# A shared pool of eight PSUM banks, one-instruction Q evacuation and ordered loads in a fused attention and token-MLP kernel

## The chip, the cores and the metric

The kernel runs on one core of a Trainium2 chip. The metric is the device time of one execution in microseconds (us), lower is better. Three runs of the kernel before gave a median of 272.15 us (271.37 to 272.38). A core has five engines that run beside each other, each with its own queue worked off in order: TensorE (PE, matrix products), VectorE (DVE), ScalarE (ACT), GpSimd (POOL) and SyncE (SP, which issues most DMAs). PE writes its results into PSUM, eight banks of 128 partitions x 512 fp32; ACT and DVE read them from there. The profile writes PEld for PE's weight loads.

## What is computed

```python
def _A_ref(x, wqkv, wo):                      # B, S, D = 1, 2048, 512
    H = 32; Dh = D // H; W = 256
    q, k, v = split(x @ wqkv)                 # 32 heads of 16
    scores = q @ k.T * (Dh ** -0.5)
    mask = (i - j >= 0) & (i - j < W)         # a causal band of 256
    p = softmax(where(mask, scores, -1e9))
    return (p @ v) @ wo

def _B_ref(x, w1, b1, w2, b2):                # F = 1376, mixing over the tokens
    h = layernorm(x)
    u = gelu(einsum("bsd,sf->bdf", h, w1) + b1)
    return transpose(einsum("bdf,fs->bds", u, w2) + b2)

g = sigmoid((x * gate_w).sum(-1))
return g * _A_ref(x) + (1 - g) * _B_ref(x)
```

x is 2048 x 512 in bf16 and both branches read the same x.

## The kernel before, in words

The work is a list of tasks. Each has a name, the engines that could do it with a planned cost, tasks it depends on, a priority and the buffers it takes and uses. `arrange` (L56) plays the tasks through once, at build time, with these costs, and the order it finds is the program: every engine works its own part off in that order, and waits by semaphores where data or a buffer are not ready. `copy_out` (L307) tasks may go to ACT or DVE, whichever is free first in the plan.

The tasks, by their names in the text:

- Loads: x in four pieces, `wqk` and `wv` (the two parts of wqkv), w1 in four, wo. x and w1 are issued by SP (L229, L242, L247), wqkv by ACT (L232, L237). w2 lies in the same SBUF space as w1, so its four loads (L622, L624) follow the last u chain.
- Transposes of x (`xt`, L334) into a PSUM bank, copied to XT by DVE.
- Projections (`project`, chains of four 512-column matmuls at L356): K and V are copied out by one instruction each (L311 on ACT, L315 on DVE). Q is copied twice out of the same bank, once times the parity mask of even heads and once of odd heads, into the two halves of QZ (L313 on ACT, L317 on DVE).
- Attention, in 32 groups of a query block `qb` (128 rows) and a half of the heads, each over up to three key blocks: 90 **score groups** (L457, eight matmuls) that write two tiles of 1024, two **exponentials** each (L474, ACT), a mask on DVE (L483, diagonal) or POOL (L492), and 16 value products a key block (L512) into one bank. DVE normalizes with L527 and L534, PE transposes back (L548), DVE copies (L552).
- Token MLP: eleven **u** chains of 16 matmuls each (L356, gp<-h,wb), bias and GELU on ACT and DVE (L589 to L611); sixteen **y** chains of 11 (L356, gp<-ug,wb), a biased copy on ACT (L637); sixteen **a** chains (attention times wo), the last product with the gate on DVE (L645), and the output DMA (L650).

PSUM is split once and for all: three tiles `sp` of two banks for the scores and two tiles `gp` of one bank for everything else, that is for transposes, projections, value products, u, y and a. The framework sets all waits from the tiles that the instructions touch.

Of the kernel before, what the change touches and what calls it, by code (L numbers as in the profile page):

```python
# [13 lines left out]
class Buf:  # L14


    def __init__(self, ring):
        self.ring = ring
        self.index = None
        self.users = 0  # L20
        self.end = 0.0
# [10 lines left out]


class Task:
    def __init__(self, name, engines, emit, deps=(), prio=50.0, lat=None, takes=(), uses=(), at=0.0):
# [10 lines left out]
        self.at = at  # L46
# [3 lines left out]
        self.ready = at  # L50
# [5 lines left out]
def arrange(tasks, patience):  # L56

    for t in tasks:
        t.left = len(t.deps)
        for d in t.deps:  # L60
            d.next.append(t)
# [11 lines left out]
    while len(order) < len(tasks):  # L73
        best = None
        for e, cands in waiting.items():
            found = []
            for t in cands:
                start = max(free[e], t.ready)
                need = {}
                for b in t.takes:  # L80
                    need[b.ring] = need.get(b.ring, 0) + 1
                for ring, n in need.items():
                    times = sorted(x for x in ring.avail if x is not None)
                    start = max(start, times[n - 1]) if len(times) >= n else None
                    if start is None:
                        break
                if start is not None:
                    found.append((start, t))
# [18 lines left out]
        for b in t.takes:  # L107
            ring = b.ring
            b.index = min(
                (i for i, x in enumerate(ring.avail) if x is not None), key=lambda i: ring.avail[i]  # L110
            )
            ring.avail[b.index] = None
        for b in t.takes + t.uses:
            b.users -= 1
            b.end = max(b.end, t.done)
            if not b.users:
                b.ring.avail[b.index] = b.end
        order.append(t)
        for n in t.next:
            n.left -= 1  # L120
            n.ready = max(n.ready, t.done)
# [4 lines left out]
def kernel(  # L126
# [33 lines left out]
    psum = ctx.enter_context(tc.tile_pool(name="psum", bufs=1, space=bass.MemoryType.PSUM))  # L160
# [34 lines left out]
    def ring(name, n, shape, dtype, space):  # L195
        pool = psum if space == "psum" else sb
        return Ring(name, [pool.tile(shape, dtype, name=f"{name}{i}") for i in range(n)])

    sp = ring("sp", 3, [P, 1024], FP32, "psum")
    gp = ring("gp", 2, [P, 512], FP32, "psum")  # L200
    et = ring("et", 5, [P, 2048], BF16, "sb")
    st_ = ring("stats", 2, [P, nc.vector.BN_STATS_DIM], FP32, "sb")
    ufr = ring("uf", 2, [P, D], FP32, "sb")
# [482 lines left out]
```

## Time and profile before

| | |
|---|---|
| median of three runs | 272.15 us |
| the profiled execution's own time | 274.25 us |
| its span (first to last instruction) | 272.2 us |
| matmuls (and as many weight loads) | 2968 |
| granted TensorE clock, mean | 0.962 |
| exponentials on ACT (L474) | 180, 171.6 us busy |
| bytes read from HBM | 15.47 MB |

The page gives the busy time of each engine, the granted clock in forty slices (in tenths of full speed), the chain that ended last, and groups of instructions with what ended the idle time ahead of them. Matmuls overlap, and their ends are modelled, so PE's rate is better read from the distance between starts. Granted clock by slice:

```profile
PEclk9689979799997999999989999999999999999999
```

The dips below 9 stand in the first slices and here and there up to the middle.

### The profile page before, as it was taken

Reading aid. Unit: us, or ns where it says so; the run is one execution under the profiler, and the core shown is the slowest. Engines: PE = TensorE matmul, PEld = TensorE weight load, DVE = VectorE, ACT = ScalarE, POOL = GpSimd, SP = SyncE. Lnnn points to the kernel's source line nnn. Section 1 sums busy time; section 2 is a strip of 40 time slices with the busy share of each in tenths; the row PEclk is TensorE's granted clock in tenths of the full one; section 3 lists DMA queues with packets and bytes.
Section 4 is the critical chain, followed back from the end, with each engine's and each line's share of the span. In section 5 each row is a group of like instructions: output and inputs, shape, how many; then the busy total and the mean of one; then the engine's idle time right before and its main releaser. Section 6 shows DMA issues by size and latency. Waiting matters only on the chain.

```text
span 272.2 us, 6817 instructions
## 1 busy us (share of the span) xinstructions
PE 239.9 (88%) x2968; PEld 118.4 (43%) x2968; DVE 145.8 (54%) x256; ACT 214.2 (79%) x255; POOL 68.5 (25%) x50
## 2 busy tenths in 40 slices
PE   5588888888989999998798989899998989899894
PEld 1243443434455455444433534445454444444431
DVE  0679977785566554758524574525425253443222
ACT  0239969689988977999569899999999999997221
POOL 8300403041340222131202221133333322222000
PEclk9689979799997999999989999999999999999999
DMA  6999600000000000000000992001001010101001
GB/s 212 214 386 404 235 0 2 1 2 0 2 2 2 0 2 0 2 2 2 1 0 4 363 411 60 0 2 41 4 19 39 5 39 2 41 0 41 22 19 58
DMA packets 9757, 18.00 MB, mean 66 GB/s; under 512 B 672, under 2 KB 5792, under 8 KB 9728
## 3 DMA queue, kind: packets, MB, share of 16 engines
q1 hardware_dynamic: 8512, 15.99, 16.5%
q10 hardware_dynamic: 1056, 1.57, 2.0%
q8 instruction: 23, 0.38, 0.6%
q0 software_dynamic: 160, 0.01, 0.5%
q14 instruction: 6, 0.05, 0.1%
HBM read 15.47 MB, written 2.10 MB: 65 GB/s over the span
## 4 chain that ended last, share of the span: by engine, by line
PE 56%; ACT 20%; DVE 15%; issue 4%; DMA 4%; DVEq 0%; ACTq 0%
PE gp L356 41%; ACT et L474 12%; PE sp L457 7%; PE gp L512 7%; DMA wqkv<-in_A_wqkv_dram 4%; DVE QZ L317 3%; DVE et L483 3%; ACT QZ L313 3%; ACT bp L637 2%; DVE h L423 2%; DVE on L534 2%; DVE ug L611 1%; ACT uf L589 1%; DVE rd L527 1%; PE gp L548 1%
## 5 line engine op out<-in xcount | busy, mean ns | idle before, releaser
L474 ACT ACTIVATE et<-sp 128x1024 bf16<-128x1024 f32 x180 | 171.6, 1045 | 4.2 <-PE sp L457 2.7
L492 POOL TENSOR_SCALAR_AFFINE_SELECT et<-et 128x2048 bf16<-128x2048 bf16 x28 | 56.6, 2021 | 151.7 <-ACT et L474 131.7
L512 PEld LDWEIGHTS <-et 128*128 128x128 bf16 x1440 | 46.1, 96 | 23.6 <-issue 14.2
L483 DVE TENSOR_TENSOR et<-et,mask 128x2048 bf16<-128x2048 bf16 x32 | 39.1, 1223 | 31.5 <-ACT et L474 31.2
L512 PE MATMUL gp<-VA,et 128*128 128x17 bf16 x1440 | 48.2, 171 | 4.2 <-DVE QZ L317 1.1
L356 PE MATMUL gp<-h,wb 128*128 128x512 bf16 (+1 forms) x176 | 47.6, 386 | 0.0
L356 PE MATMUL gp<-ug,wb 128*128 128x512 bf16 (+1 forms) x176 | 44.5, 379 | 2.7 <-DVE on L534 2.6
L356 PEld LDWEIGHTS <-wb 128*128 128x128 bf16 (+2 forms) x352 | 29.9, 98 | 35.2 <-issue 10.9
L356 PE MATMUL gp<-XT,wqkv 128*128 128x512 bf16 x128 | 38.1, 420 | 8.1 <-DMA wqkv<-in_A_wqkv_dram 2.3
L457 PE MATMUL sp<-QZ,KT 32*128 32x256 bf16 x720 | 41.3, 277 | 3.5 <-ACT et L474 1.3
L457 PEld LDWEIGHTS <-KT 32*128 32x128 bf16 x720 | 13.3, 92 | 37.1 <-issue 35.8
L637 ACT ACTIVATE bp<-gp,c,c 128x512 f32<-128x512 f32 x16 | 12.4, 779 | 16.5 <-PE gp L356 16.1
L356 PE MATMUL gp<-wqkv,XT 128*128 128x512 bf16 x64 | 19.3, 407 | 3.8 <-ACT QZ L313 2.5
L527 DVE RECIPROCAL rd<-gp 128x16 f32<-128x16 f32 x32 | 8.1, 254 | 26.0 <-PE gp L512 15.2
L356 PEld LDWEIGHTS <-wqkv 128*128 128x128 bf16 x128 | 11.9, 103 | 22.8 <-issue 13.0
L313 ACT ACTIVATE QZ<-gp,par 128x512 bf16<-128x512 f32 x18 | 12.2, 692 | 10.5 <-DVE QZ L317 6.2
L356 PE MATMUL gp<-wo,xo 128*128 128x512 bf16 x64 | 17.7, 377 | 1.8 <-ACT bp L637 1.0
L645 DVE SCALAR_TENSOR_TENSOR ot<-gp,gg,bp 128x512 bf16<-128x512 f32 x16 | 11.9, 748 | 13.7 <-PE gp L356 12.4
L317 DVE TENSOR_SCALAR QZ<-gp,par 128x512 bf16<-128x512 f32 x14 | 10.5, 750 | 15.2 <-ACT QZ L313 8.8
L594 DVE TENSOR_TENSOR t<-uf 128x512 f32<-128x512 f32 (+1 forms) x11 | 8.1, 738 | 12.3 <-ACT uf L589 12.3
L534 DVE TENSOR_TENSOR on<-gp,rd 128x256 bf16<-128x256 f32 x32 | 13.6, 424 | 1.1
L406 DVE BATCH_NORM_STATS2 stats<-xo 128x6 f32<-128x512 bf16 x16 | 10.4, 681 | 5.5 <-DMA xo<-in_A_x_dram 5.5
(49 smaller groups left out, 129.8 us busy)
## 6 DMA issues: line engine op xcount, KB each, us to landing
wb<-in_B_w_dram SPq DMA_DIRECT2D x4, 1376.0 KB, 17.1
wb<-in_B_w_dram SPq DMA_DIRECT2D x3, 1536.0 KB, 8.0
xo<-in_A_x_dram SPq DMA_DIRECT2D x4, 512.0 KB, 12.9
out_dram<-ot SPq DMA_DIRECT2D x16, 128.0 KB, 1.7
wqkv<-in_A_wqkv_dram ACTq DMA_DIRECT2D x1, 1024.0 KB, 9.8
wqkv<-in_A_wqkv_dram ACTq DMA_DIRECT2D x1, 512.0 KB, 13.3
wo<-in_A_wo_dram SPq DMA_DIRECT2D x1, 512.0 KB, 16.3
wb<-in_B_w_dram SPq DMA_DIRECT2D x1, 512.0 KB, 11.6
```

Of the source, the lines that this page charges most:

```text
L313: nc.scalar.activation(out_(), in_(), ACT.Copy, scale=scale)
L317: nc.vector.tensor_scalar(out=out_(), in0=in_(), scalar1=scale, scalar2=None, op0=ALU.mult)
L356: nc.tensor.matmul(buf(b)[:rows, :], lhsT=lhsT, rhs=rhs, start=(j == 0), stop=(j == n - 1))
L457: nc.tensor.matmul(buf(b2[r // 2])[:, (r % 2) * 512 + kk * 256:(r % 2) * 512 + kk * 256 + 256], lhsT=KT[32 * r:32 * r + 32, (kb // 4) % NK ...
L474: lambda j=j, b2=b2, e=e: nc.scalar.activation(out=buf(e)[:, j * 1024:(j + 1) * 1024], in_=buf(b2[j])[:], func=ACT.Exp, scale=SCALE),
L483: lambda e=e: nc.vector.tensor_tensor(out=buf(e)[:].rearrange("p (n q) -> p n q", q=P), in0=buf(e)[:].rearrange("p (n q) -> p n q", q=P), ...
L492: lambda e=e: nc.gpsimd.affine_select(out=buf(e)[:], in_=buf(e)[:], pattern=[[0, 16], [-1, P]], compare_op=ALU.is_gt, fill=0.0, base=0, ch ...
L512: nc.tensor.matmul(buf(o)[:, hl * DV:(hl + 1) * DV], lhsT=buf(e)[:, col:col + 128], rhs=VA[:, kb, head, :], start=(first and hl == 0), sto ...
L527: lambda rd=rd, o=o: nc.vector.reciprocal(out=buf(rd)[:], in_=buf(o)[:, 0:16 * DV].rearrange("p (h d) -> p h d", d=DV)[:, :, DH]),
L534: lambda rd=rd, o=o, ob=ob, hf=hf: nc.vector.tensor_tensor(out=buf(ob)[:, hf * 256:(hf + 1) * 256].rearrange("p (h d) -> p h d", d=DH), in ...
L637: lambda bp=bp, b=b, qb=qb: nc.scalar.activation(buf(bp)[:], buf(b)[:], ACT.Identity, bias=c2[:, qb:qb + 1], scale=c1[:, qb:qb + 1]),
L645: lambda bp=bp, b=b, ot=ot, qb=qb: nc.vector.scalar_tensor_tensor(out=buf(ot)[:], in0=buf(b)[:], scalar=gg[:, qb:qb + 1], in1=buf(bp)[:], ...
```

## The change

The eight PSUM banks become one pool, `Banks`. A score group takes two aligned pairs of banks out of all eight, everything else takes a single bank out of banks 4 to 7; pairs are taken from the low end and singles from the high end, by preference one whose neighbour is in use. `ps0` to `ps3` are the four pairs and `pb0` to `pb7` the single banks, two names for the same memory. The framework does not know that these overlap, so the kernel sets the waits itself: the first instruction of a task waits for the last instruction of the task that held each of its banks before, where that ran on another engine.

Other edits: Q is evacuated by one DVE instruction that reads the bank twice by a stride of zero and multiplies by both parity columns. All loads of x and wqkv are issued by SP, in the order x0, wqk, x1, wv, x2, x3. A small ACT instruction at the start brings the activation table in. In the planner, the exponential is priced at 0.905 in place of 0.96; a score group may not start ahead of the first exponential of the group before it (`after`); and a K or Q chain, and no longer its copy, waits for the readers of the K or Q that it replaces.

```diff
+class Banks(Ring):
+    def when(self, bufs):
+        a = self.avail
+        if bufs[0].size == 2:
+            times = sorted(
+                max(a[i], a[i + 1]) for i in range(0, len(a), 2) if a[i] is not None and a[i + 1] is not None
+            )
+        else:
+            times = sorted(x for i, x in enumerate(a) if x is not None and i in bufs[0].banks)
+        return times[len(bufs) - 1] if len(times) >= len(bufs) else None
+
+    def take(self, bufs, start):
+        a = self.avail
+        for b in bufs:
+            if b.size == 2:
+                free = [i for i in range(0, len(a), 2) if a[i] is not None and a[i + 1] is not None]
+                b.index = min(free, key=lambda i: (max(a[i], a[i + 1]) > start, i))
+                a[b.index] = a[b.index + 1] = None
+            else:
+                free = [i for i in b.banks if a[i] is not None]
+                b.index = min(
+                    free, key=lambda i: (a[i] > start, a[i ^ 1] is not None and a[i ^ 1] <= start, -i)
+                )
+                a[b.index] = None
...
-    sp = ring("sp", 3, [P, 1024], FP32, "psum")
-    gp = ring("gp", 2, [P, 512], FP32, "psum")
+    ps = Banks("ps", [0.0] * 8)
+    base = nc.psum_base
+    pairs = [nc.alloc_psum_tensor(f"ps{i}", [P, 1024], FP32) for i in range(4)]
+    top = nc.psum_base
+    nc.psum_base = base
+    singles = [nc.alloc_psum_tensor(f"pb{i}", [P, 512], FP32) for i in range(8)]
...
+    ANY = (4, 5, 6, 7)
+    def bank(banks=ANY):
+        return ps.use(1, banks)
...
+    load_x(0)
+    dwk = load_w("wqk", 0, 2 * D, 0.005)
+    load_x(1)
+    dwv = load_w("wv", 2 * D, 3 * D, 0.015)
+    load_x(2)
+    load_x(3)
...
+    add("table", {"ACT": 1.4}, lambda: nc.scalar.activation(th[:, 0:1], eps[:, 0:1], ACT.Exp), [k0], prio=0)
...
-                q = []
-                for p in range(2):
-                    q.append(copy_out(
-                        f"qc{k}_{i}{p}", lambda k=k, p=p: QZ[:, i % NQ, p, k, :], lambda b=b: buf(b)[:],
-                        [t, k4] + free_q.get((k, i - NQ), []), 4, b, 0.53, scale=par[:, p:p + 1],
-                    ))
+                q = [add(
+                    f"qc{k}_{i}", {"DVE": 1.25},
+                    lambda k=k, b=b: nc.vector.tensor_tensor(
+                        out=QZ[:, i % NQ, :, k, :], in0=buf(b)[:, None, :].to_broadcast([P, 2, SB]),
+                        in1=par[:][:, :, None].to_broadcast([P, 2, SB]), op=ALU.mult,
+                    ),
+                    [t, k4], 4, uses=[b],
+                )]
...
-            b2 = [sp.use(), sp.use()]
+            b2 = [ps.use(2), ps.use(2)]
...
-            s = add(f"s{qb}.{hf}.{kb}", {"PE": 0.40}, emit_s, need, 1 + 0.001 * slot, takes=b2)
+            s = add(f"s{qb}.{hf}.{kb}", {"PE": 0.40}, emit_s, need, 1 + 0.001 * slot, takes=b2, after=prev)
...
-            t.emit()
+            made = t.emit()
...
+            first, final = made[0].ins, made[-1].ins
+            for b in t.takes + t.uses:
+                if b.ring is not ps:
+                    continue
+                for i in range(b.index, b.index + b.size):
+                    for engine, ins in last[i]:
+                        if engine != t.engine:
+                            tc.add_manual_dep(
+                                first, ins.name,
+                                mybir.DependencyInfo(mybir.DependencyClass.Sync, mybir.DependencyReason.DATA),
+                                reason="psum bank",
+                            )
+                    last[i] = [(t.engine, final)]
```

Since costs and buffers feed the planner, the whole order is new. Three places follow. First, the head of SP's queue, before (ACT issues wqkv beside it, in two DMAs):

```order
L229 DMA xo<-in_A_x_dram 128x4x512
L242 DMA xo<-in_A_x_dram 128x4x512 x3
L247 DMA wb<-in_B_w_dram 128x4x1376 x4
L249 DMA wo<-in_A_wo_dram 128x4x512
```

and in the changed kernel:

```order
L293 DMA xo<-in_A_x_dram 128x4x512
L298 DMA wqkv<-in_A_wqkv_dram 128x4x1024
L293 DMA xo<-in_A_x_dram 128x4x512
L298 DMA wqkv<-in_A_wqkv_dram 128x4x512
L293 DMA xo<-in_A_x_dram 128x4x512 x2
L311 DMA wb<-in_B_w_dram 128x4x1376 x4
```

The two wqkv loads now stand in the one queue, behind x0 and x1.

Second, ACT in the first third of the program, before (KT, QZ are copies out of a projection; sp0 to sp2 are the three score tiles):

```order
L474 ACTIVATE et3_96<-sp1_89 128x1024
L313 ACTIVATE QZ_69<-gp0_91,par_76 128x512
L474 ACTIVATE et3_96<-sp2_90 128x1024
L474 ACTIVATE et4_97<-sp0_88 128x1024
L313 ACTIVATE QZ_69<-gp0_91,par_76 128x512
L474 ACTIVATE et4_97<-sp1_89 128x1024
L474 ACTIVATE et0_93<-sp2_90 128x1024
L311 ACTIVATE KT_68<-gp0_91 128x512
```

and in the changed kernel:

```order
L547 ACTIVATE et2_87<-ps0 128x1024
L547 ACTIVATE et2_87<-ps1 128x1024
L547 ACTIVATE et3_88<-ps0 128x1024
L547 ACTIVATE et3_88<-ps3 128x1024
L376 ACTIVATE VA_67<-pb5 128x32x16
L547 ACTIVATE et4_89<-ps0 128x1024
L376 ACTIVATE KT_65<-pb4 128x512
L547 ACTIVATE et4_89<-ps1 128x1024
```

No Q copy stands on ACT any more, here or elsewhere. On DVE the Q evacuations now stand as one instruction each, at the same stage:

```order
L459 TENSOR_TENSOR QZ_66<-pb6,par_73 128x2x512
L377 CAST KT_65<-pb7 128x512
L459 TENSOR_TENSOR QZ_66<-pb5,par_73 128x2x512
L377 CAST KT_65<-pb4 128x512
L491 TENSOR_SCALAR h_62<-xo_58,mv_79,rstd_80 128x512
```

Four K and Q evacuations in a row stand here where DVE had statistics and h products (L406, L423) between them before.

Third, ACT late in the program, beside the y chains, before:

```order
L474 ACTIVATE et0_93<-sp1_89 128x1024
L474 ACTIVATE et0_93<-sp2_90 128x1024
L474 ACTIVATE et1_94<-sp0_88 128x1024
L474 ACTIVATE et1_94<-sp1_89 128x1024
L474 ACTIVATE et2_95<-sp2_90 128x1024
L474 ACTIVATE et2_95<-sp0_88 128x1024
```

and in the changed kernel:

```order
L547 ACTIVATE et0_85<-ps0 128x1024
L547 ACTIVATE et0_85<-ps1 128x1024
L547 ACTIVATE et1_86<-ps0 128x1024
L716 ACTIVATE bp0_103<-pb7,c2_84,c1_83 128x512
L547 ACTIVATE et1_86<-ps1 128x1024
L547 ACTIVATE et2_87<-ps0 128x1024
L547 ACTIVATE et2_87<-ps1 128x1024
```

Before, the score tiles go round in threes, so that a score group overlaps the second exponential of the one before it. Now both exponentials of one group read the pairs 0 and 1, and the next group takes the same two pairs.

210 lines of the change are left out of this document (118 added, 92 removed).

## Prediction

> **What bounds the kernel now.** I read the page first (busy shares, chain), then busy time in five stretches that I cut at events, then who waits for whom, then single rows for durations.
>
> ```profile
> PE 239.9 (88%) x2968; PEld 118.4 (43%) x2968; DVE 145.8 (54%) x256; ACT 214.2 (79%) x255; POOL 68.5 (25%) x50
> ...
> PE 56%; ACT 20%; DVE 15%; issue 4%; DMA 4%; DVEq 0%; ACTq 0%
> ```
>
> TensorE (PE) is the busiest engine and holds most of the chain, but ScalarE (ACT) and VectorE (DVE) hold 35% of the chain between them: no engine is saturated from end to end. So I cut the span: at the first exponential (20.17), at the issue of the w2 loads, when the last u matmul is done (150.88), at the first y matmul (176.07) and at the end of the last exponential (250.10).
>
> ```profile
> 0.00:20.17 20.17, 13.04 (x74) 5.79 (x75) 9.56 (x24) 3.85 (x6) 8.27 (x16) 0.83 0.95 269
> 20.17:150.88 130.71, 117.48 (x1462) 57.18 (x1462) 86.97 (x153) 111.19 (x136) 30.11 (x19) 0.95 0.10 37
> 150.88:176.07 25.19, 22.73 (x332) 12.01 (x330) 13.66 (x22) 23.45 (x31) 6.01 (x3) 1.00 0.56 219
> 176.07:250.10 74.03, 69.51 (x989) 35.53 (x989) 30.95 (x52) 71.87 (x80) 23.81 (x12) 1.00 0.06 20
> 250.10:272.20 22.10, 17.12 (x121) 7.89 (x118) 4.67 (x8) 3.82 (x6) 0.24 (x1) 0.99 0.10 34
> ```
>
> Columns: stretch, its length, busy PE, PEld, DVE, ACT, POOL, then granted clock. From 176 to 250 ACT is 97% busy (71.87 of 74.03): there it is the bound, and in the last 22 us it is nearly empty (3.82), because PE still has y matmuls left. From 20 to 151 neither is: PE is idle 13.2 us and ACT 19.5 us. What PE waits for after 20.17 us:
>
> ```profile
> PE gp L356 <- DVE on L534: 4.3, 8, 0.7
> PE gp L356 <- ACT QZ L313: 4.2, 5, 1.3
> PE gp L356 <- DVE QZ L317: 1.7, 3, 0.7
> PE gp L356 <- DVE xo L552: 1.5, 2, 0.9
> PE sp L457 <- ACT et L474: 1.3, 4, 0.5
> PE gp L512 <- DVE QZ L317: 1.1, 1, 1.1
> PE gp L356 <- ACT bp L637: 1.0, 2, 0.5
> ```
>
> A chain at L356 or a value product at L512 reads none of what these DVE and ACT instructions write; it waits because they were the last readers of one of the two `gp` banks. All shown rows but the exponential's (L474) are of this kind: 13.8 us. This is what the change aims at. ACT's own holes come from the same place:
>
> ```profile
> DVE QZ L317 <- ACT QZ L313: 8.8, 7, 2.6
> ACT QZ L313 <- DVE QZ L317: 6.2, 6, 1.7
> ACT QZ L313 <- PE gp L356: 4.2, 4, 2.0
> ```
>
> The two halves of one Q evacuation never run beside each other: DVE waits for ACT or ACT for DVE, though they write different halves of QZ. What they share is the bank they read. 10.4 us of ACT's idle time stand before its Q copies.
>
> **Prices.** These rows give the durations:
>
> ```profile
> L474 ACT ACTIVATE et<-sp 128x1024 bf16<-128x1024 f32 x180 | 171.6, 1045 | 4.2 <-PE sp L457 2.7 <-PE gp L512 0.9
> ...
> L637 ACT ACTIVATE bp<-gp,c,c 128x512 f32<-128x512 f32 x16 | 12.4, 779 | 16.5 <-PE gp L356 16.1
> ...
> L313 ACT ACTIVATE QZ<-gp,par 128x512 bf16<-128x512 f32 x18 | 12.2, 692 | 10.5 <-DVE QZ L317 6.2 <-PE gp L356 4.2
> ...
> L317 DVE TENSOR_SCALAR QZ<-gp,par 128x512 bf16<-128x512 f32 x14 | 10.5, 750 | 15.2 <-ACT QZ L313 8.8 <-PE gp L356 6.3
> ...
> L534 DVE TENSOR_TENSOR on<-gp,rd 128x256 bf16<-128x256 f32 x32 | 13.6, 424 | 1.1
> ...
> 210.11 0.40 PE L457 MATMUL sp<-QZ,KT 32*128 32x256 bf16 x8
> 210.44 1.90 PE L356 MATMUL gp<-ug,wb 128*128 128x512 bf16 x8
> 212.27 0.40 PE L457 MATMUL sp<-QZ,KT 32*128 32x256 bf16 x8
> ...
> 244.71 0.55 PE L512 MATMUL gp<-VA,et 128*128 128x17 bf16 x16 [0.18 <-DVE ot L645]
> 245.12 0.59 PE L356 MATMUL gp<-wo,xo 128*128 128x512 bf16 x2
> ```
>
> From start to start PE takes 0.33 us for a score group (210.11 to 210.44), 0.23 for a 512-column matmul (1.83 for eight) and 0.41 for 16 value products (244.71 to 245.12). An exponential costs ACT 171.6/180 = 0.95.
>
> **Q evacuation.** 18 ACT and 14 DVE instructions go, 16 of 1024 elements on DVE come. ACT loses 12.2 us of work and the waits above. No row shows the new form. Below, two halves cannot cost less than one, 0.75; above, four times the 256-element broadcast product (L534) is 1.70. Twice 0.75 less one instruction's fixed part (some 0.2) gives 1.3, and I take that, nearest to L317, which reads the same bank: 16 x 1.3 = 20.8 against 10.5, so DVE gains 10 us of work. Its total of 156 is far from the span, but much of it comes early (rivals).
>
> **A, to the first exponential.** The loads now stand in one queue in the order x0, wqk, x1, wv, x2, x3.
>
> ```profile
> 2.00:4.00 2.00, 2.00 (x6) 0.76 (x5) 0.00 (x0) 0.00 (x0) 2.00 (x3) 1.00 0.79 206
> 4.00:6.00 2.00, 0.85 (x2) 0.00 (x0) 0.00 (x0) 0.00 (x0) 2.00 (x3) 1.00 1.04 354
> 6.00:8.00 2.00, 0.73 (x13) 0.74 (x14) 0.76 (x2) 0.00 (x0) 1.77 (x1) 1.00 1.11 283
> 8.00:10.00 2.00, 0.34 (x7) 0.16 (x3) 2.00 (x6) 0.79 (x1) 0.00 (x0) 0.75 0.99 170
> 10.00:12.00 2.00, 1.35 (x4) 0.54 (x5) 1.35 (x4) 0.49 (x1) 0.49 (x2) 0.50 1.19 171
> 12.00:14.00 2.00, 2.00 (x6) 0.66 (x5) 0.00 (x0) 0.57 (x1) 0.75 (x1) 0.50 1.10 329
> ...
> 10.65 5.30 PE L356 MATMUL gp<-XT,wqkv 128*128 128x512 bf16 x12 [2.31 <-DMA wqkv<-in_A_wqkv_dram]
> ...
> 20.17 1.94 ACT L474 ACTIVATE et<-sp 128x1024 bf16<-128x1024 f32 x2 [1.16 <-PE sp L457]
> ```
>
> The last column is GB/s. x0 and wqk are 1.57 MB. The engines had moved 0.41 MB by 4 us, 1.12 by 6, 1.57 by 7.6, but shared over four loads, so wqk landed at 10.65. In order it lands near 8.2 (estimate: 7.6 and some landing time). Then PE does eight projection matmuls at half clock (5.30/12 = 0.44 each), 16 transposes of x1, eight more matmuls, 16 transposes of x2 (its bytes, 3.1 MB in all, are there by about 14.5), two matmuls and the score group, the second eight partly at full clock: 8.2 + 3.5 + 1.1 + 2.4 + 1.1 + 0.9 = 17.2. **A = 17.2**, before 20.2. The bounds are 16 and 20.2 (no gain).
>
> The Trainium skill (TensorE: Matmul & The Clock Gate, "What's actually happening") has the half clock begin after about 3.4 us of idle PE and end after as long busy. The rows' clock of 0.50 at 10 to 14 us came with two gaps of 2.4 and 2.3 us instead, so this trace is stricter than the page; by either, the new order still leaves a gap ahead of wqk, and I keep the half clock.
>
> **B, first exponential to last u.** In the new order this stretch holds, counted against the old, 24 more projection matmuls, three more score groups, five more value groups and one transpose group: 24 x 0.23 + 3 x 0.33 + 5 x 0.41 + 0.2 = 8.8 us. PE: 117.5 + 8.8 = 126.3 busy. ACT: ten Q copies less (6.9), eight exponentials more (7.6), other copies about even: 112. So PE becomes the bound here. Of its idle 13.2 us, the bank waits should go, because singles now have four banks and the planner counts each of them; I leave 5 for score groups that wait for exponentials and for the early DVE load. **B = 131.3**, against 130.7 with less work in it. Bounds: 128 (2 idle) and 139.5 (the old 13.2).
>
> **C, last u to first y.** w2 overwrites w1, so the loads go after the last u:
>
> ```profile
> 150.88 3.74 SPq L622 DMA_DIRECT2D wb<-in_B_w_dram  x3
> 154.83 0.35 SPq L624 DMA_DIRECT2D wb<-in_B_w_dram  x1
> ...
> wb<-in_B_w_dram SPq DMA_DIRECT2D x1, 384.0 KB, 11.8
> ...
> 176.07 0.59 PE L356 MATMUL gp<-ug,wb 128*128 128x512 bf16 x2
> ...
> 267.69 1.03 PE L356 MATMUL gp<-wo,xo 128*128 128x512 bf16 x4
> ```
>
> The last piece lands at 154.83 + 11.8 = 166.6, 15.8 after the issue, yet the first y started 25.2 after it, since 48 projection matmuls stood ahead of it. In the new order 20 stand there, with 19 exponentials and three small ACT instructions (1.9 us): 19 x 0.95 + 1.9 = 19.9, above 15.8. **C = 19.9**; the DMA cannot bind unless it takes 4 us longer.
>
> **D, first y to the end of PE.** Before: 176.07 to 268.7 (267.69 + 1.03), 92.6 us, PE busy 69.5 + 17.1 = 86.6. The new order has five score groups, six value groups and a transpose group less here: 86.6 - 1.7 - 2.5 - 0.2 = 82.2. ACT has 57 exponentials and 16 biased copies of 0.78, 66.6, so PE binds where ACT did, and the empty ACT tail shrinks: 27 y matmuls follow the last score group instead of 55. With 2 idle, **D = 84.2**. Bounds 82 and 92.
>
> The added wait lies in this stretch. A score group takes two bank pairs at once and its first matmul waits for both; behind it on PE stand y matmuls, for which the biased copies and DVE's last product wait. While four singles are out only pairs 0 and 1 are left, so a group must wait for *both* exponentials of the group before, where three rotating pairs made it wait only for the first. By the buffers that the order gives, this is so for 36 of the 90 groups, 16 of the 28 here. What hides it is PE's own work: 84.2/28 = 3.0 us per group, against a loop of 0.4 + 2 x 0.95 and two short handovers, about 2.4.
>
> **E, the end:** the final product and the output, 272.2 - 268.7 = 3.5, unchanged.
>
> The ACT table load moves ahead of the first copy, and stood in idle time before; costs in the planner and the start rule for score groups act only through the order counted above. More statistics and h products stand late on DVE, before the first u, which needs all of them; that is in the DVE rival.
>
> **Sum:** 17.2 + 131.3 + 19.9 + 84.2 + 3.5 = 256.1 as a span, against 272.2. The profiled execution took 274.25, 2.05 above its span; the median shown, 272.15, lies 2.1 below that. The two cancel: **256**.
>
> **Rivals.**
> - **The waits move instead of going** (0.16). PE stays in order, and where a bank wait ends, a wait for the exponential or the mask begins. For: ACT is 85% busy in B (111.2 of 130.7), so PE has little lead. Against: only 1.3 us of PE waits are on exponentials now. With the old idle times, B = 139.5 and D = 88.2: 268.
> - **DVE bounds the first 80 us** (0.09). Up to the first u DVE has 12 of the 16 Q products, nine K casts and all h. At 1.70 per product that adds 12 x 0.4 = 5 us where it is already 67% busy on the mean (86.97 of 130.7): 261.
> - **The loads do not land earlier** (0.07): A = 20.2, 259. The queue order is only an order of issue.
> - **Steady clock** (0.08). The clock in B was 0.95 without a single wait of 3.4 us. If the short bank waits cause that, their end lets PE run B at 1.00: 0.05 x 131 = 6.5 less, 249.5. The Trainium skill (same page, "A second HAM failure mode: psum-queue depth-cycling") blames such short stalls; the 0.95 beside waits of at most 1.3 us agrees, but one run does not show the cause.
> - **Slower: the score groups' double wait** (0.06). If the 36 groups lose the cover of one exponential each, that is 36 x 0.95 = 34 us, 15 of it in D: 290. Slower than before begins when over half of it (17.5 us) is exposed. For: over half the groups of D have only two pairs. Against: the loop of 2.4 is shorter than PE's 3.0.
>
> **How the numbers follow.** The forecast has 0.54, from 250 to 262. The range takes in the steady clock with B at its low bound (246) and stops at the moved waits (268); outside lie the slower case, part of the moved waits and a run with no idle at all, about 0.15. A measurement tells about 0.5% from no change, 1.4 us. Faster 0.88: all but the slower case and a part of the moved waits; within 0.5% 0.05; slower 0.07.
>
> **What would show it.** Right: the first exponential near 17; no PE wait on Q copies, and those on L534's and L552's successors under 4 us; ACT without gaps before Q; w2 issued near 148; the last exponential some 10 us before PE ends. Wrong: PE waits on the exponential of 10 us or more (double wait or moved waits), DVE over 95% busy from 20 to 80 us, a first exponential at 20, or a w2 issue after 155.

## The result and the profile after

The changed kernel takes **254.92 us** (median of 4 runs, 254.41 to 255.54), the kernel before 271.76 us beside it: ratio 0.9382, 95% interval 0.9348 to 0.9416. The forecast was 256, from 246 to 268. The profiled execution of the changed kernel took 255.54 us for a span of 253.7. That of the kernel before took 274.25, 2.5 above the median beside it, so the spans compared below lie further apart (18.5 us) than the medians (16.8).

The page of the changed kernel: busy shares, busy tenths of PE and the granted clock in 40 slices, and the chain that ended last by engine:

```profile
PE 228.2 (90%) x2968; PEld 113.3 (45%) x2968; DVE 157.8 (62%) x259; ACT 204.2 (80%) x237; POOL 69.8 (28%) x50
...
PE   7399988997889998998989997399999999999993
...
PEclk9989999999999999999999999559999999999999
...
PE 61%; ACT 16%; DVE 13%; DMA 4%; issue 4%; SPq 0%; ACTq 0%; DVEq 0%
```

PE went from 88% to 90% of a shorter span. Two dips are left: one near 10 us (slice 2), one from about 155 us (slices 25 and 26), and at the second the clock falls to half. Five stretches again, cut at the first exponential, the first issue of w2, the first y and 240.20, where the last exponential is about to start:

```profile
0.00:18.17 18.17, 12.28 (x83) 6.79 (x84) 9.35 (x21) 2.68 (x5) 8.26 (x16) 0.91 0.92 256
18.17:143.55 125.38, 116.33 (x1588) 57.18 (x1586) 99.85 (x163) 111.39 (x133) 33.33 (x20) 1.00 0.12 43
143.55:169.26 25.71, 19.59 (x331) 10.67 (x332) 15.89 (x23) 23.84 (x28) 8.02 (x4) 0.79 0.60 221
169.26:240.20 70.94, 70.47 (x888) 34.05 (x885) 29.46 (x48) 62.88 (x70) 19.02 (x10) 0.98 0.07 24
240.20:253.70 13.50, 9.49 (x88) 4.57 (x86) 3.26 (x6) 3.39 (x5) 1.16 (x1) 1.00 0.11 40
```

From 169 to 240 PE is busy 70.47 of 70.94 us and ACT has room (62.88): the bound has changed hands there, since before ACT was busy 71.87 of 74.03. ACT's last row of exponentials ends at 241.37:

```profile
237.35 4.02 ACT L547 ACTIVATE et<-ps 128x1024 bf16<-128x1024 f32 x4
```

So the time behind the last exponential, in which ACT is nearly empty, shrank from 22.1 to 12.3 us. What PE waits for now:

```profile
PE ps L528 <- ACT et L547: 7.6, 10, 1.2
PE pb L393 <- DMA xo<-in_A_x_dram: 3.0, 1, 3.0
PE pb L419 <- DMA wqkv<-in_A_wqkv_dram: 1.7, 1, 1.7
...
PE pb L419 <- DVE xo L630: 1.3, 2, 0.8
...
PE pb L419 <- DVE VA L377: 1.1, 1, 1.1
...
PE ps L528 <- DVE on L610: 0.9, 1, 0.9
```

The waits on a bank whose reader is unrelated (Q copies 4.2 and 1.7, broadcast product 4.3 before) are gone or under 1.4 us each. In their place stands a wait of another kind, score groups that wait for an exponential: 7.6 us, where before it was 1.3 (value products wait 1.2 more).

The w2 loads need a correction to the forecast's mark. SyncE's issues before, without a cut, and after:

```profile
148.69 5.93 SPq L622 DMA_DIRECT2D wb<-in_B_w_dram  x4
```

```profile
143.55 5.11 SPq L701 DMA_DIRECT2D wb<-in_B_w_dram  x4
148.84 0.35 SPq L703 DMA_DIRECT2D wb<-in_B_w_dram  x1
```

The row at 150.88 that the prediction quotes came from a view cut at that time, and was not the first issue. Nor is the last u matmul done there. PE's last rows of u, before and after, end at 154.80 and 148.81, and the last piece of w2 is issued right behind them, at 154.83 and 148.84:

```profile
154.17 0.63 PE L356 MATMUL gp<-h,wb 128*96 128x512 bf16 x2
```

```profile
148.20 0.61 PE L419 MATMUL pb<-h,wb 128*96 128x512 bf16 x2
```

This touches the sum. The prediction counted how the two orders differ up to the last u, and for C the 19 exponentials and 20 projection matmuls behind the last u, which the trace has just so. But it took B's old length only up to 150.88. The 3.95 us from there to 154.83 stand in neither term. With them its sum is 260.1 and not 256.1. Step by step, in the profiled spans:

| step | before | forecast | after |
|---|---|---|---|
| A, to the first exponential | 20.2 | 17.2 | 18.2 |
| B, to the last w2 issue (forecast 131.3, + 3.95) | 134.7 | 135.3 | 130.7 |
| C, to the first y | 21.2 | 19.9 | 20.4 |
| D, to the end of PE | 92.6 | 84.2 | 80.9 |
| E, the end | 3.5 | 3.5 | 3.5 |
| sum | 272.2 | 260.1 | 253.7 |

Of the 18.5 us that the span lost, 11.7 were lost in D.

### The profile page after: what moved, and what is told of

Its sections match the earlier page's. It is cut to its first block, busy times and chain, and to the rows that moved or that the text cites. A ratio compares the mean times of both kernels' runs of the same rounds, so it can differ in the third digit from the quotient of the medians.

```text
span 253.7 us, 6794 instructions
## 1 busy us (share of the span) xinstructions
PE 228.2 (90%) x2968; PEld 113.3 (45%) x2968; DVE 157.8 (62%) x259; ACT 204.2 (80%) x237; POOL 69.8 (28%) x50
## 4 chain that ended last, share of the span: by engine, by line
PE 61%; ACT 16%; DVE 13%; DMA 4%; issue 4%; SPq 0%; ACTq 0%; DVEq 0%
PE pb L419 41%; ACT et L547 12%; PE pb L587 9%; PE ps L528 8%; DMA xo<-in_A_x_dram 4%; DVE h L491 2%; DVE QZ L459 2%; DVE et L557 2%; DVE t L678 1%; DVE t L673 1%; ACT uf L668 1%; PE pb L393 1%; DVE KT L377 1%; PE pb L624 1%; ACT t L685 1%
## 5 line engine op out<-in xcount | busy, mean ns | idle before, releaser
L547 ACT ACTIVATE et<-ps 128x1024 bf16<-128x1024 f32 x180 | 173.0, 1033 | 18.9 <-PE ps L528 17.6
L587 PE MATMUL pb<-VA,et 128*128 128x17 bf16 x1440 | 49.9, 171 | 2.9 <-ACT et L547 1.2
L557 DVE TENSOR_TENSOR et<-et,mask 128x2048 bf16<-128x2048 bf16 x32 | 38.9, 1218 | 14.1 <-ACT et L547 13.8
L419 PE MATMUL pb<-h,wb 128*128 128x512 bf16 (+1 forms) x176 | 46.1, 380 | 1.3 <-DVE xo L630 1.3
L419 PE MATMUL pb<-ug,wb 128*128 128x512 bf16 (+1 forms) x176 | 47.1, 386 | 0.0
L528 PE MATMUL ps<-QZ,KT 32*128 32x256 bf16 x720 | 37.0, 281 | 9.8 <-ACT et L547 7.6
L724 DVE SCALAR_TENSOR_TENSOR ot<-pb,gg,bp 128x512 bf16<-128x512 f32 x16 | 12.0, 750 | 36.8 <-PE pb L419 19.9
L419 PE MATMUL pb<-XT,wqkv 128*128 128x512 bf16 x128 | 33.3, 385 | 1.7 <-DMA wqkv<-in_A_wqkv_dram 1.7
L459 DVE TENSOR_TENSOR QZ<-pb,par 128x1024 bf16<-128x1024 f32 x16 | 19.5, 1219 | 4.1 <-PE pb L419 4.0
L419 PE MATMUL pb<-wo,xo 128*128 128x512 bf16 x64 | 18.9, 379 | 0.7 <-ACT bp L716 0.7
L419 PE MATMUL pb<-wqkv,XT 128*128 128x512 bf16 x64 | 17.2, 380 | 1.4 <-DVE VA L377 1.1
L419 PEld LDWEIGHTS <-wqkv 128*128 128x128 bf16 x128 | 10.6, 99 | 13.9 <-issue 1.9
L610 DVE TENSOR_TENSOR on<-pb,rd 128x256 bf16<-128x256 f32 x32 | 13.6, 424 | 1.1
## 6 DMA issues: line engine op xcount, KB each, us to landing
wo<-in_A_wo_dram SPq DMA_DIRECT2D x1, 512.0 KB, 16.2
wb<-in_B_w_dram SPq DMA_DIRECT2D x1, 512.0 KB, 13.8
```

The lines of the kernel that those rows point to most:

```text
L419: nc.tensor.matmul(buf(b)[:rows, :], lhsT=lhsT, rhs=rhs, start=(j == 0), stop=(j == n - 1))
L459: lambda k=k, b=b: nc.vector.tensor_tensor(out=QZ[:, i % NQ, :, k, :], in0=buf(b)[:, None, :].to_broadcast([P, 2, SB]), in1=par[:][:, :, N ...
L528: made.append(nc.tensor.matmul(buf(b2[r // 2])[:, (r % 2) * 512 + kk * 256:(r % 2) * 512 + kk * 256 + 256], lhsT=KT[32 * r:32 * r + 32, (k ...
L547: lambda j=j, b2=b2, e=e: nc.scalar.activation(out=buf(e)[:, j * 1024:(j + 1) * 1024], in_=buf(b2[j])[:], func=ACT.Exp, scale=SCALE),
L557: lambda e=e: nc.vector.tensor_tensor(out=buf(e)[:].rearrange("p (n q) -> p n q", q=P), in0=buf(e)[:].rearrange("p (n q) -> p n q", q=P), ...
L587: made.append(nc.tensor.matmul(buf(o)[:, hl * DV:(hl + 1) * DV], lhsT=buf(e)[:, col:col + 128], rhs=VA[:, kb, head, :], start=(first and h ...
```

## Experiments

The first six undo parts. My first theory was that of the prediction: waits on banks go, and each part brings its share. The rival: the change only orders PE's work differently against ACT's, and the parts work together or not at all. A third theory is luck: any new order of the planner might have done as well.

**e1: fixed banks.** Pairs only from banks 0 to 5, singles only 6 and 7; the rest of the change stays.

```
-    ANY = (4, 5, 6, 7)
+    ANY = (6, 7)
...
-                free = [i for i in range(0, len(a), 2) if a[i] is not None and a[i + 1] is not None]
+                free = [i for i in range(0, 6, 2) if a[i] is not None and a[i + 1] is not None]
...
```

> The changed kernel with its banks split as before: score pairs only from banks 0 to 5, singles only 6 and 7. All else is kept, and the planner lays the order out anew. Theory 1 (PE's waits for one of two single banks were the loss): they come back, 10 us or more of PE waits on the last readers of banks 6 and 7, and the time is 263 to 268. Theory 2 (ACT relief by the Q evacuation is the gain): at most 258. Theory 3 (any new order by the planner would have done, by luck): about 255, no telling of the sign.

Measured: 271.34 us, ratio 1.000 (0.9967 to 1.0032): the whole gain is gone, more than any of the three theories had said. Waits on the readers of banks 6 and 7 come back, some 9 us in all, but the largest wait of PE is on exponentials (10.7 us). Its stretches from 110 to 140 us and to the end:

```profile
110.00:140.00 30.00, 27.73 (x187) 11.69 (x186) 17.00 (x25) 13.98 (x20) 2.45 (x2) 1.00 0.00 1
...
235.00:269.60 34.60, 28.66 (x169) 11.54 (x166) 6.93 (x11) 6.82 (x9) 0.92 (x1) 1.00 0.10 35
```

PE is busy in both, ACT under half and then a fifth: 88 y matmuls follow the last score group in its order (55 before, 27 after). The planner has pushed PE's other work behind the scores. With this planner the pool is needed for the gain.

**e2: two Q copies**, one per half, on either engine, in place of the one product.

```
-                q = [add(
-                    f"qc{k}_{i}", {"DVE": 1.25},
...
+                    tq = add(f"qc{k}_{i}{p}", {"DVE": 0.67, "ACT": 0.70}, emit, [t, k4], 4, uses=[b])
```

> The changed kernel with Q evacuated twice, as before, on ACT or DVE. Theory 1: ACT gets some 12 us of work back and waits beside DVE for the same bank, but PE is the bound in most of the span: 257 to 261. Theory 2: 265 or more. Theory 3: about 255.

Measured: 266.13 us, 0.9748 (0.9658 to 0.9838), as the second theory had it. ACT has 212.6 us of work again where the changed kernel has 204.2, and the halves still wait for each other with eight banks:

```profile
ACT QZ L462 <- DVE QZ L463: 6.0, 8, 1.7
```

**e3: the old loads** (ACT's queue for the weights, the old order and the old rates in the planner).

```
+    dwk = load(
+        "wqk",
+        lambda: nc.scalar.dma_start(wqkv[:, :, 0:2 * D], A_wqkv[:, 0:2 * D].rearrange("(c p) n -> p c n", p=P)),
+        1024, q="ACT",
+    )
...
-    dwk = load_w("wqk", 0, 2 * D, 0.005)
```

> The changed kernel with the loads issued as before: wqkv by ACT beside x by SP. All theories: the first exponential comes 2 us later, at 20.2, and the time is 256 to 258; if the head is hidden by what follows, 255.

Measured: 262.48 us, 0.9655 (0.9594 to 0.9716). That is 7.6 us more than the changed kernel, above all forecasts, while the first exponential comes only 0.5 us later (18.67 for 18.17).

**e4: the old price of an exponential.** A number in the planner, no instruction.

```
-                    f"e{qb}.{hf}.{kb}.{j}", {"ACT": 0.905},
+                    f"e{qb}.{hf}.{kb}.{j}", {"ACT": 0.96},
```

> The changed kernel with the exponential priced at 0.96 in the planner again, so that only the order changes. Theories 1 and 2: 253 to 258, since the chip's own durations are the same. Theory 3: a change of more than 3 us either way, as large as that of a real edit.

Measured: 265.19 us, 0.9781 (0.9707 to 0.9855), 10.3 more than the changed kernel: theories 1 and 2 missed, and the third had it. No y matmul follows its last score group, and its last 20 us look like this:

```profile
240.00:260.00 20.00, 11.22 (x208) 6.22 (x208) 6.85 (x12) 12.85 (x14) 6.01 (x3) 0.61 0.03 11
```

PE is half idle at a clock of 0.61: it has little but scores and value products left, and they wait for exponentials. ACT is the bound there. It works on with one short gap up to 253.3 us:

```profile
245.88 7.44 ACT L547 ACTIVATE et<-ps 128x1024 bf16<-128x1024 f32 x8 [0.47 <-PE pb L587]
```

**e5: everything undone but the waits set by hand.**

```
-    ANY = (4, 5, 6, 7)
+    ANY = (6, 7)
...
-                    f"e{qb}.{hf}.{kb}.{j}", {"ACT": 0.905},
+                    f"e{qb}.{hf}.{kb}.{j}", {"ACT": 0.96},
...
```

> The changed file with every edit undone but the waits that the kernel sets itself: fixed banks, two Q copies, wqkv on ACT, no early table load, 0.96, the start rule and the early waits for K and Q readers off. If the hand-set waits cost or gain nothing by themselves: 270 to 273, like the kernel before. If they are dearer than the framework's: 274 or more; if cheaper, under 269.

Measured: 271.88 us, 1.0029 (0.9996 to 1.0062). Who sets the waits makes no difference that these runs can tell.

**e6: the pool alone**, with the start rule for score groups and the early waits for K and Q readers kept.

```
-                    f"e{qb}.{hf}.{kb}.{j}", {"ACT": 0.905},
+                    f"e{qb}.{hf}.{kb}.{j}", {"ACT": 0.96},
...
```

(and the two Q copies of e2, the loads of e3, no early table load)

> The pool (with the start rule and the early waits, without which the planner finds no order) as the only edit: two Q copies, wqkv on ACT, no table load, 0.96. Its order leaves no y matmul after the last score group, where before has 55, fixed banks 88 and the changed kernel 27. Theory 1 in its new form (the pool lets y chains hold banks beside the attention, so PE's work does not pile up at the end): faster than before, 262 to 268, with an end that waits for ACT instead. If the pool gains only together with the Q edit: 270 to 273.

Measured: 273.57 us, 1.0071 (1.0042 to 1.01): no gain from the pool alone. Its largest PE wait, and its last 21 us:

```profile
PE ps L528 <- ACT et L547: 15.1, 21, 1.4
```

```profile
250.00:271.40 21.40, 12.60 (x212) 6.69 (x210) 7.84 (x14) 11.69 (x13) 4.63 (x3) 0.58 0.06 20
```

The bank waits are small here too (the largest 1.8 us), and 15.1 us of waits on exponentials have come in their place, with a starved end. So removing bank waits gains nothing by itself.

**e7: the small loads later.** Four element-wise loads of gate and bias vectors, 7.7 KB, go out from POOL at 1.87 to 4.32 us; here they wait for x3 in the plan and go out from 10.26 us. PE, ACT and DVE keep their order; POOL's own changes with the move.

```
-    k3 = add("smalls", {"POOL": 4.0}, small_loads, [k2], prio=2, lat=6.0)
+    k3 = add("smalls", {"POOL": 4.0}, small_loads, [k2, dx[3]], prio=2, lat=6.0)
```

> The changed kernel with the four element-wise bias loads issued by POOL after its first power, some 10 us in, and the order of PE, ACT and DVE kept. If these loads slow the DMA engines at 8 to 12 us: x1 lands near 10 instead of 12.3, the DMA rate at 8 to 12 us is over 300 GB/s, the first exponential comes at 16 to 17, and the time falls by 1 to 2 us. If not: x1 at 12 as before, no change.

Measured: **251.21 us**, 0.9264 (0.9218 to 0.931), the fastest of all. The head of the changed kernel, two of its stretches (the last number is GB/s) and its PE rows, then the same of e7:

```profile
8.00:10.00 2.00, 1.37 (x7) 0.40 (x5) 0.92 (x4) 0.60 (x1) 1.24 (x2) 1.00 0.96 174
10.00:12.00 2.00, 0.00 (x0) 0.00 (x0) 0.63 (x1) 0.00 (x0) 0.00 (x0) 0.93 1.23 141
```

```profile
7.48 1.89 PE L419 MATMUL pb<-XT,wqkv 128*128 128x512 bf16 x8 [1.66 <-DMA wqkv<-in_A_wqkv_dram]
12.34 1.89 PE L393 MATMUL pb<-ident,xo 128*128 128x128 bf16 x16 [2.98 <-DMA xo<-in_A_x_dram]
```

```profile
8.00:10.00 2.00, 2.00 (x23) 1.40 (x22) 1.63 (x5) 0.60 (x1) 0.92 (x2) 1.00 1.10 351
10.00:12.00 2.00, 2.00 (x14) 0.75 (x12) 2.00 (x4) 0.36 (x1) 2.00 (x3) 1.00 1.10 349
```

```profile
9.09 1.06 PE L393 MATMUL pb<-ident,xo 128*128 128x128 bf16 x16
```

PE starts on x1 3.25 us earlier (9.09 for 12.34) and no longer waits for it, though SyncE issues it at 1.85 us in both. The first exponential comes at 13.80 and the time falls by 3.7: the forecast had the mechanism, with 16 to 17 and 1 to 2 us too little of it. The DMA engines are busy in both cases (share near 1), but with the small loads in flight they move 141 to 174 GB/s, without them 350. The Trainium skill (DMA: Bandwidth & Descriptors, "Issuing engines are not separate DMA queues") says that transfers from all engines run on the same 16 DMA engines and interleave; that agrees, since loads from POOL's queue slow those from SyncE's.

**e8: y in pieces.** A y chain may start when the first piece of w2 and the first ug tile are there, and the planner expects the pieces 3.3 us apart, not 4.5.

```
-        dw2.append(add(f"w2_{i}", {"SP": 0.1}, emit, m1, 0.1 * i, lat=2.2 + 4.5 * (i + 1)))
+        dw2.append(add(f"w2_{i}", {"SP": 0.1}, emit, m1, 0.1 * i, lat=2.2 + 3.3 * (i + 1)))
...
-        b, t = chain(f"y{qb}", mms, dw2 + ugr, 60 + qb)
+        b, t = chain(f"y{qb}", mms, ugr[:1], 60 + qb, more=[(edges[n_], dw2[n_]) for n_ in range(4)] + list(enumerate(ugr)))
```

> The changed kernel with y chains that wait, matmul by matmul, for the GELU piece and the w2 piece that they read, rather than for all of both, and w2 planned to land at 3.3 us a piece. The y chains then start at score group 55 instead of 62, and none is left after the last. If the gap ahead of the first y (PE idle 6.1 us and half clock) is a loss of its own: 248 to 252, PE busy through 150 to 170 us. If ACT binds there and at the end: 254 to 257.

Measured: 256.83 us, 0.944 (0.9403 to 0.9477), in the second range. The hole in the middle is filled, and a hole of the same kind is at the end:

```profile
140.00:160.00 20.00, 19.96 (x240) 9.87 (x237) 16.01 (x23) 18.04 (x22) 5.92 (x3) 1.00 0.76 283
...
240.00:254.40 14.40, 7.37 (x120) 4.30 (x120) 4.94 (x9) 4.79 (x6) 2.00 (x1) 0.62 0.06 19
```

So far the second theory had this form: PE must keep other work for its end, else it runs dry and at half clock beside the last exponentials. The last four runs test it.

**e9: e4 with the last two y chains held back** until the last score group, 22 y matmuls.

```
-                    f"e{qb}.{hf}.{kb}.{j}", {"ACT": 0.905},
+                    f"e{qb}.{hf}.{kb}.{j}", {"ACT": 0.96},
...
+            slots.append(s)
...
-        b, t = chain(f"y{qb}", mms, dw2 + ugr, 60 + qb)
+        b, t = chain(f"y{qb}", mms, dw2 + ugr + ([slots[-1]] if qb >= 14 else []), 60 + qb)
```

> The changed kernel with the old price of an exponential (0.96), as in e4 (265.2 us), but the y chains of the query blocks 14 and 15 may only start after the last score group: 22 y matmuls then follow it, where e4 has none and the changed kernel 27. Theory 1 (the loss of e4 sits at the end: no y matmuls are left for PE while the last exponentials run, and PE falls to the half clock): the last 20 us are as full as in the changed kernel, 256 to 260 us. Theory 2 (the old price spoils the order throughout, the end only shows it): 264 us or more.

Measured: 267.26 us, 0.9791 (0.9726 to 0.9855), no gain on e4, as the second theory had it. Behind the last exponential PE is about as full now as in the changed kernel (busy 9.35 of 13.57 us, there 8.32 of 12.33), and the hole stands just ahead of it:

```profile
240.00:260.00 20.00, 15.11 (x235) 8.34 (x236) 6.26 (x12) 12.51 (x14) 4.77 (x3) 0.57 0.03 8
```

**e10: pool and new price**: e6 with one line set back.

```
-                    f"e{qb}.{hf}.{kb}.{j}", {"ACT": 0.96},
+                    f"e{qb}.{hf}.{kb}.{j}", {"ACT": 0.905},
```

> The pool with the start rule and the early waits, as in e6 (273.6 us), and the new price of an exponential (0.905); two Q copies, the old loads and the table load in its old place stay. No y matmul follows the last score group in its order, as in e6. Theory 1 (the empty end costs the time, whatever stands before): 266 to 273 us, with PE idle and at a low clock in the last 20 us. Theory 2 (pool and price together are what the change is worth): 257 to 262 us, so that Q evacuation and loads only add 3 to 7 us.

Measured: 267.12 us, 0.9804 (0.9748 to 0.986), 6.5 less than e6. The time lies where the first theory, the empty end, had put it, but e9 had just taken that reason away.

**e11: e7 and e8 together, with the last two y chains held.** The lines are against e8:

```
-        b, t = chain(f"y{qb}", mms, ugr[:1], 60 + qb, more=[(edges[n_], dw2[n_]) for n_ in range(4)] + list(enumerate(ugr)))
+        b, t = chain(f"y{qb}", mms, ugr[:1] + ([slots[-1]] if qb >= 14 else []), 60 + qb, more=[(edges[n_], dw2[n_]) for n_ in range(4)] + list(enumerate(ugr)))
```

> e7 (small loads late, 251.2 us) and e8 (y chains may start piece by piece, 256.8 us) together, and with the y chains of the query blocks 14 and 15 held back until the last score group, so that 22 y matmuls follow it, where e8 has none. Theory 1 (e8 only moved its gain to the end): the middle gap before the first y goes and the end stays full, 246 to 249 us. Theory 2 (ACT bounds what lies between, PE has nothing to win in the middle): 250 to 253 us, the same as e7.

Measured: 254.54 us, 0.9358 (0.9313 to 0.9404), outside both forecasts: slower than e7 alone. The middle is full (19.72 of 20 us from 140 to 160), and the hole has come out at 220 to 240, where ACT is 98% busy:

```profile
220.00:240.00 20.00, 11.47 (x226) 6.21 (x226) 7.53 (x12) 19.52 (x22) 7.34 (x4) 0.68 0.05 15
```

**e12: e4 with y spread over the last score groups** (chain i after group 60 + 2i).

```
-                    f"e{qb}.{hf}.{kb}.{j}", {"ACT": 0.905},
+                    f"e{qb}.{hf}.{kb}.{j}", {"ACT": 0.96},
...
+            slots.append(s)
...
-        b, t = chain(f"y{qb}", mms, dw2 + ugr, 60 + qb)
+        b, t = chain(f"y{qb}", mms, dw2 + ugr + [slots[min(89, int(60 + qb * 2.0))]], 60 + qb)
```

> The changed kernel with the old price of an exponential (0.96), as in e4 (265.2 us), but the y chain of query block i may only start after score group 60 + 2i, so that y is spread over the last score groups instead of standing ahead of them: 23 y matmuls follow the last score group (e4 none, e9 22, the changed kernel 27), and the score groups 60 to 80 stand where they stand in the changed kernel, by PE work ahead of them. The first 60 groups keep the order of e4. Over the runs with the pool so far the time goes with the exponentials that are still left at 240 us (none in e7: 251; 2 in the changed kernel: 255; 6 in e8: 257; 10 to 14 in e2, e3, e4, e10: 262 to 267; 23 in e6: 274). Theory (PE spends its other work ahead of the score groups, so exponentials are left over at the end, where PE has nothing beside them and runs at the half clock): at most 4 exponentials left at 240 us and 255 to 260 us. Rival (e9 already held y back and gained nothing: the old price costs its time in the first 60 groups, or by PE waits that any order has): 263 us or more, with y spread and PE idle in the last third all the same.

Measured: 264.83 us, 0.9724 (0.9674 to 0.9773), no different from e4, and ten exponentials are left at 240 us, not four. My theory of the end fell. PE is nearly full from 180 us to the end, and idle for a third of the stretch ahead of it:

```profile
160.00:180.00 20.00, 13.03 (x216) 5.90 (x214) 5.45 (x9) 17.60 (x20) 6.01 (x3) 0.59 0.01 2
```

PE's idle time in all is 29.5 us of the span (261.8 less 232.3), in e4 29.6 (261.6 less 232.0). Holding y back moved the hole by 80 us and left its size.

One count goes with the time over all these runs: the exponentials done in the first 140 us. Busy time and, in the bracket, the count, in the kernel before and in the changed kernel:

```profile
0.00:140.00 140.00, 81.19 (x85) 0.93 0.22 72
```

```profile
0.00:140.00 140.00, 93.22 (x97) 0.99 0.22 72
```

| kernel | exponentials by 140 us | y after the last score group | median us |
|---|---|---|---|
| e6 pool alone | 81 | 0 | 273.6 |
| before | 85 | 55 | 271.8 |
| e5 all undone | 87 | 55 | 271.9 |
| e1 fixed banks | 89 | 88 | 271.3 |
| e10 pool and price | 90 | 0 | 267.1 |
| e2, e4, e9, e12 | 92 each | 0, 0, 22, 23 | 266.1, 265.2, 267.3, 264.8 |
| e3 old loads | 96 | 0 | 262.5 |
| changed kernel | 97 | 27 | 254.9 |
| e8, e11 | 98 each | 0, 22 | 256.8, 254.5 |
| e7 small loads late | 101 | 27 | 251.2 |

Among the kernels with a pool the time falls with this count, from 81 to 101 by 22.4 us, 1.1 us for each exponential (one takes 0.95), and hardly with the column beside it. It isn't the whole: e3 has one less than the changed kernel and takes 7.6 us more.

ACT's own time shows where the rest lies. A span is the time up to the first exponential, ACT's busy and idle time from there to the end of the last one, and the time behind it (all in the profiled executions; that of e2 is 3.5 us under its median). The two middle stretches, cut at 140 us, in the kernel before and then in the changed kernel (ACT is the fourth busy time):

```profile
20.17:140.00 119.83, 108.07 (x1392) 53.55 (x1392) 82.06 (x146) 101.19 (x124) 28.11 (x18) 0.94 0.10 39
140.00:250.10 110.10, 101.65 (x1387) 51.17 (x1386) 49.52 (x79) 105.32 (x122) 31.83 (x16) 1.00 0.18 65
```

```profile
18.17:140.00 121.83, 112.81 (x1539) 55.42 (x1538) 96.85 (x158) 107.93 (x128) 33.33 (x20) 1.00 0.12 44
140.00:241.37 101.37, 94.75 (x1270) 46.85 (x1266) 48.35 (x76) 91.36 (x104) 28.19 (x14) 0.93 0.21 74
```

| kernel | to the first exponential | ACT busy | ACT idle to 140 us | ACT idle after 140 us | behind the last exponential |
|---|---|---|---|---|---|
| before | 20.2 | 206.5 | 18.6 | 4.8 | 22.1 |
| changed kernel | 18.2 | 199.3 | 13.9 | 10.0 | 12.3 |
| e7 small loads late | 13.8 | 199.3 | 14.0 | 9.6 | 12.3 |
| e1 fixed banks | 18.7 | 194.5 | 20.4 | 2.0 | 33.9 |
| e2 two Q copies | 16.5 | 208.6 | 12.8 | 14.2 | 8.9 |
| e3 old loads | 18.7 | 203.0 | 14.5 | 16.4 | 8.8 |
| e4 old price | 17.5 | 204.2 | 15.4 | 16.2 | 8.3 |
| e6 pool alone | 18.5 | 209.1 | 18.9 | 16.3 | 8.5 |
| e10 pool and price | 18.2 | 209.1 | 13.9 | 14.6 | 8.9 |

Against the kernel before, ACT's idle time did not shrink (23.4 and 23.9 in all). The gain lies in what ACT no longer does (7.2 us; it copied Q for 12.2), in the time behind the last exponential (9.8) and in the head (2.0). With fixed banks PE's other work runs on behind the last exponential. In e2, e3, e4, e6 and e10 little runs there, but ACT has more to do and idles more, and the added idle time lies mostly after 140 us (e6 alone has much of it earlier too). So the count at 140 us is no cause by itself: in e2 and e10 it is lower because ACT also copies Q by then, with no more idle time, and e3 and e4 lose most of theirs later.

## Why the prediction was right, step by step

**The time and the sign** came out: 256 forecast, 254.9 measured. That it came so near was partly luck. With the 3.95 us that its sum left out the forecast would have been 260; against that sum A and C came 1.0 and 0.5 longer, and B and D 4.6 and 3.3 shorter. Of the 18.5 us the largest part is D's, and D was right in its mechanism: fewer score groups are left, PE binds where ACT did. PE is busy 80.0 us there (70.47 + 9.49) for the 82.2 forecast, and idle 1 for 2: 80.9 for 84.2.

**A was mis-sized by 1.0.** wqk landed in time for a projection at 7.48 (forecast 8.2), and the first eight projections ran at full clock (1.89 us), not at half. The forecast took it for granted that x1 follows; it came only at 12.34, behind the small loads (e7). The half clock then came at 12 to 14 us instead.

**B was mis-sized by 4.6**, counted to the last issue. PE was idle there for 9.1 us, not 5, but busy for only 121.6, some 8.6 under the forecast (126.3 and 3.95), at a granted clock of 1.00 where 0.95 stood before. This is the rival of the steady clock, given 6.5 us, come true in part. The clock differs from one execution of the same kernel to the next: beside e5 to e8 that of the kernel before goes from 0.962 (271.7 us of span) to 0.994 (269.2), and the profiled execution, with 0.962, is at the low end. So a part of this may be the one execution that the forecast was worked out from. That the bank waits had pulled the clock down is not borne out: e5, with the old bank waits (4.3 us each on its two largest sources), has a clock of 1.00 from 18 us on as well.

**C was right in its mechanism**, 19.9 forecast and 20.4 measured. ACT binds there: it has the 19 exponentials and three small instructions that were counted and is busy 18.8 of the 20.4 us. Eight exponentials follow each other without a gap, while the score groups on PE wait for them:

```profile
157.19 7.40 ACT L547 ACTIVATE et<-ps 128x1024 bf16<-128x1024 f32 x8
```

```profile
159.17 0.61 PE L528 MATMUL ps<-QZ,KT 32*128 32x256 bf16 x8 [1.05 <-ACT et L547]
161.00 0.61 PE L528 MATMUL ps<-QZ,KT 32*128 32x256 bf16 x8 [1.21 <-ACT et L547]
162.82 0.61 PE L528 MATMUL ps<-QZ,KT 32*128 32x256 bf16 x8 [1.22 <-ACT et L547]
```

One group every 1.83 us, two exponentials: the 20 projection matmuls had been used up by 154 us, and PE has nothing but scores and values. Over half of PE's waits on exponentials stand here (4.0 of the 7.6 us), and they cost ACT little (it idles 1.6 us in C). The double wait of the slower rival did not show where it was feared: in D the profile has no wait of PE on an exponential. w2, landing near 148.84 + 13.9 = 162.7, did not bind.

**Rivals.** The waits moved in part: 7.6 us stand on exponentials now, under the 10 that would have told against the forecast. DVE was 93% busy from 20 to 80 us (55.82 of 60), just under the mark of 95%, and PE waited for it for 2.7 us there. One product cost less than the rival's 1.70:

```profile
L459 DVE TENSOR_TENSOR QZ<-pb,par 128x1024 bf16<-128x1024 f32 x16 | 19.5, 1219 | 4.1 <-PE pb L419 4.0
```

That is 1.22, the forecast 1.3; the 0.2 that it took off twice 0.75 for an instruction's fixed part stands in no row, and 0.28 would have been right. The first loads did land earlier.

**What the forecast had not seen** is why it came out. It priced the new order, and the order was right; it named the bank waits as what the change takes away. e6 takes most of them away and gains nothing; e1 keeps the rest of the change and gains nothing. Undone one at a time, the parts cost 16.4 (pool), 11.2 (Q), 10.3 (price) and 7.6 us (loads), 45 together, of a gain of 16.8: they aren't shares of a sum. What they share, as far as the runs show, is where PE's own work (projections, u, y) lies against the exponentials. That work is finite. Where it is used up ahead of them, PE waits for each exponential; where it is left over, it runs behind the last one beside an empty ACT; and e8, e9, e11 and e12 only chose where. That each part acts through this, and not through something else in the order that the planner then finds, is argued from the tables and not shown. Only e7 keeps the order of PE, ACT and DVE, and there the earlier head explains the gain alone: the first exponential comes 4.4 us earlier, the span is 4.7 shorter, and nothing else in its row of the table moves by more than 0.5.

Not tried: the Q product, the loads or the price without the pool, and the table load, the start rule and the early waits by themselves. Nor were prices near 0.905 tried. Since one price moved the time by 10.3 us, a part of the gain may be the luck of one order that the planner found (the third theory), and no run here tells how much. Why the lower price brings exponentials forward was not traced either.

## What to carry to other kernels

Where one engine feeds another through a loop (scores, exponentials, value products) and also has work of its own, split the span at the first and last turn of the loop and read the fed engine's busy and idle time between. Holding work back only moved the hole here: e12 has 29.5 us of idle PE for e4's 29.6. Take parts of a change away one at a time and also put them in alone: taking away any of four lost 7.6 us or more of the 16.8, and the one that was put in alone, the pool, gained nothing. Check that two terms of a sum meet at the same event. And look at what else is in flight beside the first loads, however few bytes it has.

## What the runs showed of the hardware

**Half clock without a long idle stretch.** The granted clock of the changed kernel around the waits of section C (last but two number):

```profile
155.00:157.00 2.00, 1.53 (x50) 1.12 (x46) 1.64 (x3) 2.00 (x3) 0.00 (x0) 1.00 1.02 408
157.00:159.00 2.00, 0.40 (x8) 0.15 (x8) 1.97 (x4) 2.00 (x4) 0.00 (x0) 0.87 1.08 387
159.00:161.00 2.00, 0.62 (x10) 0.14 (x11) 0.30 (x1) 2.00 (x4) 1.82 (x1) 0.50 0.38 76
```

PE was busy a fifth to a third of the time, and no single wait was over 1.22 us. The Trainium skill (TensorE: Matmul & The Clock Gate, "What's actually happening") gives one idle window of about 3.4 us as what brings the half clock; here several short waits did it. A score group then took 0.61 us where it took 0.40 at 157.72 us, and the clock was still 0.50 from 169 to 171, so the first four y matmuls took 0.47 us each for 0.23. Such waits cost more than their own length.

**7.7 KB of scattered loads halved the rate of the large ones**, 141 to 174 GB/s for 350 (e7). Moved later, they are followed by a lower rate too, 186 GB/s at 16 to 18 us for 400, but PE has no wait on a load in that run.
